# A searched step order replaced by another, for a chunked linear attention followed by a gated feed-forward layer

## The chip, the cores and the metric

The kernel runs on one core of one Trainium2 chip. The metric is the device time of one execution in microseconds. Before the change three runs took 177.21, 177.34 and 177.75 us; the median is 177.34 us.

## The reference

The first half is a recurrence over 768 positions, for 4 batches and 8 heads with 48 columns each. Each head keeps a 48 by 48 state, which decays by `w` at every position; the current position enters with its own factor `u`. The second half takes the result as 3072 rows of 384 columns through two matrix products with a gate between them.

```
for t in range(S):
    cur = einsum('bhd,bhe->bhde', u[None] * kt, vt)
    y[:, :, t] = einsum('bhd,bhde->bhe', rt, state + cur)
    state = w[None, :, :, None] * state + einsum('bhd,bhe->bhde', kt, vt)

h = x @ w_in                       # 3072 x 384 by 384 x 2048
g = where(h >= 1, h, where(h <= -1, 0, (h + 1) ** 2 / 4))
out = g @ w_out                    # 2048 x 384
```

## The kernel before

**Tiling.** The 768 positions are cut into 6 chunks of 128. The 4 batches make 2 pairs, so there are 12 groups `g` (chunk by pair), and each group has 2 units `j`, one per batch. A unit `n = 2g + j` is 128 positions of one batch with all 8 heads. Inside a chunk the recurrence is done by matrix products: R and K are scaled by powers of `w` (`Rs`, `Ks`, line 327), turned so that the columns lie on partitions, and multiplied into a 128 by 128 matrix per head (`A`, line 406). The matrix is masked to a triangle (`AT`, line 421, or on ACT and then POOL at lines 412 and 416) and multiplied with V (`Y`, line 446), and the state's part is added on PE (line 441). The term with `u` goes another way: `KU` (337), `RKU` (344), the row sum `usum` (357, or on ACT at 355 in one small instruction per head), `V2` (369), and `y` (468) adds it to `Y`. The state of a batch goes through `Sp` (432), `Tm` (476 or 484), `decay` (489, always POOL) and `sbf` (a copy to bf16).

**Turning.** Groups 0 to 2 turn R and K on PE (`T`, line 388, copied out by `TT`) and the result on PE (`X`, copied out by `xT`). From group 3 on this is done by DMA transposes, issued on SP's queue: `KRT` (line 398) for K and R, and `xT` (line 511) for a whole group.

**Feed-forward.** Each group has four quarters `q` of the 2048 inner columns. `mm1.g.q` (line 526) is 12 products of 256 columns; `relu` (534) and `square` (539) run on ACT, `gate` (544) on DVE, and `mm2.g.j.q` (line 554) is four products of 384 columns for one unit. `o` copies the sum out of PSUM, and `out` (587) stores it. The last unit is split in two (`rest`, `ends`) so that its store is short.

**Queues.** Five instruction streams run in order: PE, DVE, ACT, POOL and SP. SP issues all loads of R, K and V, all DMA transposes and nearly all stores; a step that waits there holds all behind it. POOL issues the weights: `w_in` in three transfers (line 290, columns 0 to 511, 512 to 1023, and the rest) and `w_out` in four (line 294, four tiles of 128 rows each), among its products.

**The order.** One string, `ORDER` (lines 35 to 100), lists all 715 steps; the program walks through it and appends each step's instructions to the queue of its engine. A step reads `name.args@engine:buffers~idles`. `@D`, `@P` and `@A` choose DVE, POOL or ACT where there is a choice. The digits after the colon choose the buffer: `h0` to `h2` are the PSUM tiles of two banks each that `A`, `mm1` and the transposes share, `bank0` and `bank1` the single banks. `~7` puts seven idle products of 128 columns (line 204, zeros times zeros) ahead of the step on PE; `warm.12.h.0` is twelve such products by themselves (line 608). Waits between engines follow from the order of the steps and the tiles that they share.

Of the kernel before, what the change touches and what calls it, by code (L numbers as in the profile page):

```python
# [40 lines left out]
Sp.2:1~2 load.K.2.0:2 V.1.1@A TT.3@A:0 V2.0.1@P AT.2.0:1 Tm.1@D Tm.2@D T.1:1~2 TT.1@A:1 Rs.2.0@P:2 Y.0:0~7 w_in.0
Sp.3:1~7 A.1:0 w_in.1 A.3:2 Ks.2.0@D:0 y.0:2 T.5:1 X.0:0~2 Tm.3@D V2.1.0@P:1 AT.1.1:0 AT.3.0:2 AT.1.0 Y.2:1~11
xT.0@D:0 T.4:0~4 usum.1.1@D Y.1:0 y.2:2 warm.2.h.2 Y.3:1 y.1:0 loadV.2.0:1 X.1:0~2 sbf.1@A V2.1.1@D TT.4@A:3 w_in.2
w_out.0 sbf.0@A xT.1@A V.2.0@D:3 A.4:0~4 sbf.3@A KU.2.0@D:1 RKU.2.0@P:0 mm1.0.0.0:2 mm1.0.0.1 TT.5@A:0 relu.0.0:1
y.3:0 AT.4.0:2 Sp.4:1~7 square.0.0:0 Tm.4@D:0 X.2:0~2 A.5:1~4 usum.2.0@D:1 gate.0.0:7 w_out.1 mm1.0.1.0:0 xT.2@A:1
# [20 lines left out]
gate.4.0:4 loadV.7.0:0 A.12:2 load.R.8.0:2 Tm.12@D:0 relu.4.2:1 KU.7.0@P:0 Sp.11:1 decay.9 KU.8.0@P:1 AT.12.0:0
square.4.2:0 sbf.10@A mm2.4.0.0:0 gate.4.1:5 mm1.4.3.-1:2 gate.4.2:0 A.13:0 V2.6.0@P:0 mm2.4.0.1 mm1.5.0.-1:1 out.2
Tm.11@D:1 sbf.9@A relu.4.3:1 AT.13.0:2 square.4.3:0 Y.12:1 Ks.7.0@P:0 mm2.4.0.2 KRT.K.7:0 relu.5.0:1 mm1.5.2.-1:0
square.5.0:1 y.12:0 relu.5.2:1 gate.4.3:8 square.5.2:0 Y.13:1 y.13 Rs.7.0@P:2 mm1.5.1.-1:2 mm2.4.0.3 decay.11
gate.5.0:2 RKU.7.0@P:1 o.4.0@A:0 relu.5.1:1 V.7.0@A:4 gate.5.2:9 usum.7.0@D:1 decay.12 KRT.R.7:0 mm2.4.1.0:1 mm2.4.1.1  # L70
sbf.11@A square.5.1:1 A.15:1 AT.15.0:3 A.14:0 mm2.4.1.2 Sp.13:0 RKU.8.0@P:0 V2.7.0@P:1 mm2.4.1.3 mm1.5.3.-1:1 o.4.1@A
Tm.13@D:1 load.K.9.0:0 xT.12:1 relu.5.3:0 Sp.14:1 AT.14.0:2 gate.5.1:8 loadV.8.0:0 square.5.3:0 Y.14:0 decay.13
Tm.14@D:1 mm1.6.0.-1:0 relu.6.0:0 out.4 mm1.6.1.-1:2 y.14:1 gate.5.3:3 square.6.0:1 Ks.8.0@P:1 Y.15:1 y.15 mm2.5.0.0:0
Rs.8.0@P:0 mm2.5.0.1 relu.6.1:1 Sp.15:1 usum.8.0@D:0 gate.6.0:6 square.6.1:0 KRT.K.8:0 KU.9.0@P:0 out.3 V.8.0@D:2
decay.14 mm1.6.2.-1:1 load.R.9.0:1 mm2.5.0.2 mm2.5.0.3 Ks.9.0@P:2 KRT.R.8:0 Tm.15@D:0 relu.6.2:0 square.6.2:1
o.5.0@A:0 sbf.12@A gate.6.1:0 mm1.6.3.-1:0 gate.6.2:4 xT.14:2 Sp.16:1 mm2.5.1.0:0 mm2.5.1.1 A.17:2 decay.15
load.K.10.0:0 relu.6.3:0 A.16:1 Tm.16@D:0 loadV.9.0:1 AT.17.0:2 square.6.3:0 mm2.5.1.2 mm2.5.1.3 AT.16.0:0
mm1.7.1.-1:2 o.5.1@A gate.6.3:3 decay.16 Y.16:1 RKU.9.0@P:0 sbf.15@A sbf.13@A V2.8.0@P:0 y.16:1 Y.17:0 load.R.10.0:2
relu.7.1:1 square.7.1:0 y.17 mm1.7.0.-1:1 relu.7.0:0 Sp.17:1 mm1.7.3.-1:0 mm2.6.0.0:0 gate.7.1:5 mm2.6.0.1 Tm.17@D:0
mm1.7.2.-1:2 mm2.6.0.2 Rs.9.0@P:2 usum.9.0@D:1 Ks.10.0@P:0 load.K.11.0:1 sbf.14@A KRT.K.9:0 out.5 KRT.R.9:1  # L80
square.7.0:1 xT.16:2 KU.10.0@D:1 RKU.10.0@P:1 gate.7.0:2 mm2.6.0.3 relu.7.3:0 square.7.3:0 decay.17 mm2.6.1.0:1
gate.7.3:8 V.9.0@A:0 relu.7.2:0 mm2.6.1.1 o.6.0@A:0 V2.9.0@P:0 A.19:1 A.18:0 Rs.10.0@P:1 mm2.6.1.2 mm2.6.1.3 AT.18.0:3
sbf.16@A square.7.2:0 o.6.1@A gate.7.2:9 Sp.18:0 mm1.8.0.-1:0 loadV.10.0:1 relu.8.0:0 KRT.R.10:0 Tm.18@D:0 Y.18:1
mm1.8.1.-1:2 mm2.7.0.0:0 KRT.K.10:0 mm2.7.0.1 square.8.0:1 AT.19.0:1 sbf.17@D y.18:0 loadV.11.0:0 mm2.7.0.2
usum.10.0@A:1 Y.19:1 gate.8.0:3 mm2.7.0.3 decay.18 y.19 o.7.0@D:1 A.20:0 A.21:1 mm2.7.1.0:1 xT.18:1 relu.8.1:0
AT.20.0:1 Sp.19:0 mm2.7.1.1 V.10.0@D:0 AT.21.0:3 mm1.8.2.-1:0 mm2.7.1.2 KU.11.0@P:0 square.8.1:1 sbf.18@A relu.8.2:0
gate.8.1:6 square.8.2:0 Ks.11.0@P:0 Tm.19@D:0 mm1.8.3.-1:1 out.6 Y.20:0 V2.10.0@D:0 mm2.7.1.3 mm1.9.1.-1:2 y.20:0
relu.8.3:0 gate.8.2:7 square.8.3:1 mm1.9.0.-1:0 o.7.1@D Y.21:1 mm2.8.0.0:0 y.21 load.R.11.0:2 Rs.11.0@P:1 gate.8.3:1
RKU.11.0@P:0 relu.9.1:1 relu.9.0:0 decay.19 square.9.0:0 gate.9.0:5 square.9.1:1 mm2.8.0.1 gate.9.1:8 usum.11.0@D:1
mm2.8.0.2 sbf.19@A KRT.R.11:0 KRT.K.11:0 mm2.8.1.0:1 mm2.8.0.3 mm1.9.2.-1:0 V.11.0@A:0 mm2.8.1.1 out.7 A.22:2  # L90
# [559 lines left out]
```

## Time and profile before

| | |
|---|---|
| median of the runs | 177.34 us |
| the profiled execution | 177.43 us |
| its span, first to last instruction | 175.7 us |
| mean granted TensorE clock | 0.997 |
| busy PE, DVE, ACT, POOL | 165.5, 140.4, 136.1, 103.5 us |
| HBM read and written | 20.45 and 4.72 MB |

The page gives each engine's busy time as a share of the span. Rows of the waits name the engine and line that waited, what let it go, the total, the number of times and the longest. Rows of a timeline are the start and the duration in us, the engine, the line, the operation, what it writes and reads, and the shape; a bracket names the idle time before it and what ended it. Rows of the chain are pieces of the path that ended last. "Landing" is the time from the issue of a DMA to its arrival.

### The profile page before, as it was taken

Reading aid. Unit: us, or ns where it says so; the run is one execution under the profiler, and the core shown is the slowest. Engines: PE = TensorE matmul, PEld = TensorE weight load, DVE = VectorE, ACT = ScalarE, POOL = GpSimd, SP = SyncE. Lnnn points to the kernel's source line nnn. Section 1 sums busy time; section 2 is a strip of 40 time slices with the busy share of each in tenths; the row PEclk is TensorE's granted clock in tenths of the full one; section 3 lists DMA queues with packets and bytes.
Section 4 is the critical chain, followed back from the end, with each engine's and each line's share of the span. In section 5 each row is a group of like instructions: output and inputs, shape, how many; then the busy total and the mean of one; then the engine's idle time right before and its main releaser. Section 6 shows DMA issues by size and latency. Waiting matters only on the chain.

```text
span 175.7 us, 4247 instructions
## 1 busy us (share of the span) xinstructions
PE 165.5 (94%) x1718; PEld 127.1 (72%) x1718; DVE 140.4 (80%) x181; ACT 136.1 (77%) x195; POOL 103.5 (59%) x85
## 2 busy tenths in 40 slices
...
GB/s 115 210 224 215 153 202 206 192 183 163 193 174 194 259 207 219 215 170 135 229 226 179 190 246 202 183 251 109 152 219 69 101 152 137 1 0 4 0 179 90
DMA packets 107367, 28.78 MB, mean 164 GB/s; under 512 B 100946, under 2 KB 106964, under 8 KB 107348
## 3 DMA queue, kind: packets, MB, share of 16 engines
...
q8 instruction: 13, 0.21, 0.5%
...
HBM read 20.45 MB, written 4.72 MB: 143 GB/s over the span
## 4 chain that ended last, share of the span: by engine, by line
PE 72%; DMA 16%; DVE 4%; ACT 2%; issue 2%; POOL 1%; SPq 1%; DVEq 0%
PE hp L526 29%; PE op L554 29%; DMA w_out_sb<-in_moe_w_out_dram 7%; DMA xT<-yy 5%; PE A L406 4%; DMA KT<-Ks 2%; PE Y L446 2%; DMA K<-in_k_dram 2%; PE Y L441 2%; PE Sp L432 2%; PE T L388 2%; DVE AT L421 1%; ACT TT L212 1%; POOL V L369 1%; PE Sp L204 1%
## 5 line engine op out<-in xcount | busy, mean ns | idle before, releaser
L526 PE MATMUL hp<-xT,w_in_sb 128*128 128x256 bf16 (+1 forms) x600 | 70.1, 268 | 2.0 <-DMA xT<-yy 1.6
L554 PE MATMUL op<-w_out_sb,gt 128*128 128x384 bf16 (+2 forms) x400 | 69.5, 320 | 0.4 <-DMA w_out_sb<-in_moe_w_out_dram 0.4
L544 DVE SCALAR_TENSOR_TENSOR gt<-sq,hp 128x1024 bf16<-128x1024 f32 x48 | 58.0, 1216 | 14.5 <-ACT sq L539 13.9
L526 PEld LDWEIGHTS <-w_in_sb 128*128 128x128 bf16 x600 | 55.6, 98 | 11.8 <-DMA xT<-yy 2.0
L534 ACT ACTIVATE pt<-hp 128x1024 f32<-128x1024 f32 x48 | 48.9, 1022 | 10.0 <-PE hp L526 9.4
L539 ACT ACTIVATE sq<-pt 128x1024 f32<-128x1024 f32 x48 | 50.6, 1058 | 2.0 <-DVE gt L544 0.9
L554 PEld LDWEIGHTS <-gt 128*128 128x128 bf16 x400 | 37.0, 98 | 20.5 <-issue 0.5
L421 DVE TENSOR_TENSOR AT<-A,umask 128x1024 bf16<-128x1024 f32 x22 | 26.6, 1218 | 3.1 <-PE A L406 3.0
L344 POOL TENSOR_TENSOR RKU<-R,KU 128x768 f32<-128x768 f32 (+1 forms) x11 | 18.4, 1677 | 11.1 <-DMA R<-in_r_dram 7.7
L369 POOL TENSOR_TENSOR V<-V,diag 128x768 f32<-128x768 bf16 (+1 forms) x11 | 15.9, 1442 | 8.5 <-DVE diag L357 4.7
L489 POOL TENSOR_TENSOR state<-Tm,wCm 128x384 f32<-128x384 f32 x16 | 16.7, 1041 | 6.8 <-DVE Tm L476 6.8
L327 POOL TENSOR_TENSOR Rs<-Wup,R 128x768 bf16<-128x768 f32 x8 | 14.6, 1820 | 4.8 <-issue 4.0
L327 POOL TENSOR_TENSOR Ks<-Wdn,K 128x768 bf16<-128x768 f32 x8 | 15.6, 1951 | 2.5 <-DMA KT<-Ks 1.9
L337 POOL TENSOR_TENSOR KU<-K,u_bc 128x768 f32<-128x768 f32 (+1 forms) x8 | 13.1, 1640 | 4.9 <-DVE RKU L344 3.0
L468 DVE TENSOR_TENSOR yy<-Y,V 128x384 bf16<-128x384 f32 x18 | 9.7, 554 | 6.3 <-PE Y L446 5.4
L212 ACT COPY oo<-op 128x384 f32<-128x384 f32 x18 | 8.6, 476 | 7.0 <-PE op L554 7.0
L212 ACT CAST V<-VF 128x768 bf16<-128x768 f32 (+1 forms) x10 | 7.0, 701 | 5.0 <-DMA VF<-in_v_dram 5.0
L446 PE MATMUL Y<-V,AT 128*128 128x48 bf16 x192 | 10.9, 183 | 0.0
L357 DVE TENSOR_REDUCE diag<-RKU 128x16 f32<-128x768 f32 (+1 forms) x13 | 10.6, 820 | 0.0
L446 PEld LDWEIGHTS <-AT 128*128 128x128 bf16 x192 | 9.5, 96 | 0.4
L212 ACT CAST state_bf<-state 128x384 bf16<-128x384 f32 x18 | 9.0, 509 | 0.0
L476 DVE TENSOR_TENSOR Tm<-Sp,state 128x384 f32<-128x384 f32 x16 | 8.7, 549 | 0.0
...
## 6 DMA issues: line engine op xcount, KB each, us to landing
...
w_out_sb<-in_moe_w_out_dram POOLq DMA_DIRECT2D x4, 384.0 KB, 10.2
...
```

The lines of the kernel that those rows point to most:

```text
L212: nc.scalar.copy(out, in_) if e == "A" else engines[e].tensor_copy(out, in_)
L327: engines[e].tensor_mul(of_unit(dst, j0, j1)[:, :, :, :D], rep(tab, j1 - j0), of_unit(tiles[what, g], j0, j1))
L344: engines[e].tensor_mul(of_unit(tiles["RKU", g], j0, j1), of_unit(tiles["R", g], j0, j1), of_unit(tiles["KU", g], j0, j1))
L369: engines[e].tensor_mul(tiles["V2", g][:, hs, :], tiles["V", g][:, hs, :], tiles["diag", g][:, hs].unsqueeze(2).to_broadcast([P, hs.stop - ...
L421: nc.vector.tensor_mul(t.rearrange("p i n t -> p (i n) t"), tiles.pop(("A", n)).rearrange("p i n t -> p (i n) t"), umask.unsqueeze(1).to_b ...
L446: nc.tensor.matmul(t[:, 2 * p + i, :], tiles["AT", n][:, i, p, :], tiles["V", g][:, j * H + 2 * p + i, :], start=(c == 0), stop=True, skip ...
L489: nc.gpsimd.tensor_mul(states[(g % BP) * UNITS + j], tiles.pop(("Tm", n)), wCm)
L526: nc.tensor.matmul(hp[:, f, cols], w_in_sb[:, i, n0 : n0 + P], tiles["xT", g][:, units, i, :], start=(i == 0), stop=(i == nK - 1), skip_gr ...
L534: nc.scalar.activation(tiles["pt", g, q], tiles["hp", g, q], AF.Relu, bias=0.5, scale=0.5)
L539: nc.scalar.activation(tiles["sq", g, q], tiles.pop(("pt", g, q)), AF.Square, bias=0.0)
L544: nc.vector.scalar_tensor_tensor(out=gt, in0=tiles.pop(("sq", g, q)), scalar=1.0, in1=tiles.pop(("hp", g, q)), op0=ALU.min, op1=ALU.max)
L554: nc.tensor.matmul(t, tiles["gt", g, q][:, f, j * P : (j + 1) * P], w_out_sb[:, n, cols], start=(n == 0), stop=(n == nF - 1),)
```

## The change

Only the string `ORDER` differs. It has the same 715 steps, but for the idle products: `warm.12.h.0` and two `warm.2.h.2` become `warm.6.h.1` and two `warm.2.h.0`, and the idle products ahead of steps become 81 where there were 80, at other steps. In all there are 91 instead of 96. The steps stand in another order on every queue. 43 steps have another engine, and 306 have another buffer number. The new engines, by step:

- from DVE to POOL: KU.1.0, KU.1.1, RKU.1.1, KU.2.0, Ks.3.0, Rs.3.0, Rs.4.0, KU.4.0, RKU.6.0, V2.10.0
- from POOL to DVE: KU.0.0, RKU.0.0, KU.0.1, KU.5.0, RKU.11.0, V2.11.0
- from ACT to DVE: TT.0, V.1.1, sbf.0, TT.5, V.3.0, sbf.5, sbf.10, sbf.11, sbf.14, o.5.0, usum.10.0, o.8.0, o.10.1
- from DVE to ACT: xT.0, usum.1.1, V.2.0, sbf.2, V.4.0, o.2.0, V.8.0, sbf.17, o.7.0, o.7.1, V.10.0, o.9.0, o.11.0
- from POOL to ACT: V2.1.0

The order of the first loads on SP's queue before is K.0.0, K.0.1, K.1.0, V.0.0, R.0.0, K.1.1, R.1.0, V.0.1, R.1.1, R.0.1, R.2.0, V.1.0, V.1.1, K.2.0. After it is V.1.0, V.0.0, K.0.0, R.0.0, K.0.1, K.1.0, R.0.1, R.1.0, K.1.1, V.0.1, R.1.1, V.1.1, R.2.0, K.2.0. The diff, cut to the start, the last weights and the places around four transposes:

```diff
 ORDER = """
-warm.12.h.0 bcu:1 load.K.0.0:1 lw u_bc@D load.K.0.1 bcw:0 Wdn_p:0 load.K.1.0:0 KU.1.0@D:0 loadV.0.0:1 Ks.0.0@D:1
-KU.0.0@P:1 load.R.0.0:0 Wup_p wcol:1 load.K.1.1 load.R.1.0:2 V.0.0@A:2 loadV.0.1 load.R.1.1 wCm Ks.1.0@D:2 Rs.0.0@D:1
-RKU.0.0@P:1 T.0:1~2 Ks.1.1@D TT.0@A:3 usum.0.0@D:1 load.R.0.1 Rs.1.0@D:0 Ks.0.1@D A.0:1 AT.0.1:2 Wup KU.1.1@D
...
-load.K.3.0:0 mm2.0.0.0:1 load.R.3.0:1 Tm.5@D:1 square.0.2:0 w_out.2 Ks.3.0@D:0 mm1.0.3.-1:2 w_out.3 decay.5 gate.0.2:1
...
-o.1.0@A:0 AT.6.0:2 Sp.7:1 mm1.2.2.-1:2 Tm.7@D:1 Rs.5.0@P:2 decay.7 Tm.6@D:0 Y.6:1 relu.2.0:1 Y.7:0 y.6:0 mm1.2.1.-1:1
-y.7 xT.6:1 relu.2.2:0 Ks.5.0@P:0 load.K.6.0:0 square.2.0:0 decay.6 mm2.1.1.0:0 gate.2.0:9 relu.2.1:1 mm2.1.1.1
-square.2.1:1 sbf.6@A mm2.1.1.2 mm2.2.0.0:1 Ks.4.0@P:1 Rs.4.0@D:0 gate.2.1:2 mm2.1.1.3 mm1.3.1.-1:0 mm1.3.2.-1:1
...
-o.2.1@A mm2.3.0.3 V2.4.0@P:0 Y.8:0 y.8:0 A.10:1 o.3.0@A:1 Y.9:1 Rs.6.0@P:0 A.11:2 load.K.7.0:2 sbf.8@A y.9 loadV.6.0:1
-xT.8:1 Sp.10:0 Tm.10@D:0 RKU.6.0@D:0 load.K.8.0:1 V2.5.0@P:1 decay.10 mm2.3.1.0:1 mm2.3.1.1 AT.11.0:1 Sp.9:0 mm2.3.1.2
-V.6.0@A:1 mm2.3.1.3 sbf.7@A KRT.R.6:1 mm1.4.0.-1:2 AT.10.0:0 o.3.1@A Y.10:1 Tm.9@D:1 usum.6.0@D:1 Y.11:0 relu.4.0:1
...
+loadV.1.0:1 lw loadV.0.0:0 load.K.0.0:0 load.R.0.0:2 bcu:0 u_bc@D load.K.0.1 load.K.1.0:2 load.R.0.1 bcw:1 KU.0.0@D:0
+Wdn_p:0 warm.6.h.1 wcol:0 V.0.0@A:4 V.1.0@A:2 Ks.0.0@D:2 load.R.1.0:0 Wup_p wCm load.K.1.1 RKU.0.0@D:1 Rs.0.0@D:1
+Rs.0.1@D loadV.0.1 KU.0.1@D T.0:1 TT.0@D:0 Ks.0.1@D load.R.1.1 Ks.1.0@D:0 loadV.1.1 Wdn usum.0.0@D:1 A.0:2~2
+Rs.1.0@D:0 KU.1.0@P:1 RKU.1.0@P:0 Ks.1.1@D AT.0.1:0 Sp.2:0~7 Rs.1.1@D KU.1.1@P load.R.2.0:1 Tm.2@D V.1.1@D T.2:1~4 Wup
+V.0.1@A T.1:0 RKU.0.1@P Sp.1:1 TT.2@A:1 usum.0.1@D Sp.3:0~4 RKU.1.1@P Tm.1@D Tm.3@D usum.1.0@D:0 Sp.0:1 load.K.2.0:2
+AT.0.0 Rs.2.0@P:1 A.2:1 w_in.0 TT.1@A:2 Tm.0@D AT.2.0:1 A.1:2~8 Y.0:1~16 Ks.2.0@D:2 V2.0.0@D:1 y.0:2 warm.2.h.0
+V2.1.0@A:0 AT.1.1:2 Y.2:0~2 w_in.1 AT.1.0 T.3:0~2 V2.0.1@P T.4:2 TT.3@A:3 TT.4@A:1 y.2:0 X.0:1 xT.0@A:2 Y.1:0~2
+usum.1.1@A A.3:1 y.1:2 T.5:0~8 w_in.2 KU.2.0@P:1 X.1:1~4 AT.3.0:3 X.2:0 mm1.0.0.0:2 xT.1@A w_out.0 TT.5@D:2
+RKU.2.0@P:1 xT.2@A:0 Y.3:1~4 w_out.1 V2.1.1@D y.3:2 loadV.2.0:1 A.5:1 AT.5.0:1 V.2.0@A:2 sbf.1@A mm1.0.0.1
+load.K.3.0:1 relu.0.0:1 A.4:0 Sp.5:0 X.3:1 AT.4.0:3 mm1.0.1.0:1 xT.3@A mm1.0.1.1 Tm.5@D:0 square.0.0:0 mm1.1.1.-1:0
+relu.0.1:0 load.R.3.0:1 square.0.1:1 w_out.2 Sp.4:1~7 sbf.0@D relu.1.1:1 decay.5 usum.2.0@D:0 Y.4:0~7 gate.0.0:8
+V2.2.0@P:1 Ks.3.0@P:1 mm1.1.0.-1:2 loadV.3.0:1 gate.0.1:2 y.4:1 square.1.1:1 load.K.4.0:2 Tm.4@D:1 gate.1.1:3
+mm1.0.2.-1:1 Y.5:0~4 X.4:1 mm1.0.3.-1:0 y.5:1 relu.1.0:0 w_out.3 square.1.0:0 gate.1.0:9 relu.0.2:0 KU.3.0@D:0
...
+AT.6.0:1 decay.6 o.1.0@A:1 gate.2.3:5 Y.6:1 load.R.5.0:0 KU.4.0@P:0 y.6:0 Y.7:0 load.K.5.0:0 load.R.4.0:2 mm1.2.2.-1:1
+relu.2.0:0 Rs.5.0@P:2 mm2.1.1.0:1 mm2.1.1.1 square.2.0:1 mm1.2.1.-1:2 y.7 gate.2.0:4 V.5.0@A:2 mm2.1.1.2 KU.5.0@D:1
+relu.2.2:1 sbf.5@D square.2.2:0 xT.6:1 decay.7 gate.2.2:7 relu.2.1:0 mm2.1.1.3 loadV.4.0:1 load.K.6.0:2 RKU.5.0@P:0
+o.1.1@A out.0 RKU.4.0@D:1 mm1.3.1.-1:0 Rs.4.0@P:0 square.2.1:1 KRT.K.4:0 gate.2.1:9 relu.3.1:1 Ks.5.0@P:0 usum.4.0@D:1
...
+sbf.7@A KU.6.0@P:1 mm2.3.0.1 loadV.6.0:0 A.10:2 load.K.7.0:0 A.11:1 gate.3.3:6 Rs.6.0@P:2 Y.9:1 mm2.3.0.2 y.9
+mm2.3.0.3 RKU.6.0@P:0 xT.8:2 AT.10.0:3 o.3.0@A:1 mm2.3.1.0:1 out.2 AT.11.0:2 mm2.3.1.1 Sp.10:0 Tm.10@D:1 mm2.3.1.2
+KU.7.0@P:1 KRT.R.6:0 mm2.3.1.3 o.3.1@A Sp.9:0 Tm.9@D:0 KRT.K.6:0 mm1.4.0.-1:1 V.6.0@A:1 Y.10:1 Y.11:0 decay.10
...
+square.5.2:1 loadV.7.0:1 usum.7.0@D:0 o.4.0@A:0 gate.5.0:7 mm2.4.1.1 Y.13:0 sbf.11@D V.7.0@A:3 gate.5.2:9 A.15:2 y.13
+load.R.8.0:0 A.14:0 AT.15.0:2 relu.5.1:1 square.5.1:1 AT.14.0:1 mm2.4.1.2 mm2.4.1.3 o.4.1@A V2.7.0@P:1 load.R.9.0:2
+Sp.13:0 mm1.5.3.-1:2 xT.12:1 Y.14:1 Tm.13@D:0 relu.5.3:0 Y.15:0 Rs.8.0@P:2 decay.13 gate.5.1:2 y.14:0 mm1.6.0.-1:0
...
+KRT.K.10:1 usum.10.0@D:0 mm2.7.1.0:1 square.8.0:1 Y.19:0 gate.8.1:4 loadV.11.0:0 mm2.7.1.1 gate.8.0:9 A.21:2 A.20:0
+y.19 mm2.7.1.2 relu.8.3:0 sbf.16@A Rs.11.0@P:1 Sp.19:0 load.K.11.0:2 V.10.0@A:2 sbf.17@A mm2.7.1.3 square.8.3:1
+AT.20.0:1 xT.18:2 mm1.8.2.-1:0 Tm.19@D:0 o.7.1@A Y.20:0 relu.8.2:0 gate.8.3:0 V2.10.0@P:0 mm1.9.1.-1:1 AT.21.0:3
+KRT.R.11:1 mm1.9.0.-1:2 square.8.2:1 y.20:0 decay.19 V.11.0@A:1 Ks.11.0@P:2 relu.9.1:1 KRT.K.11:1 relu.9.0:0 Y.21:1
+gate.8.2:1 KU.11.0@P:0 mm2.8.0.0:0 y.21 mm2.8.0.1 sbf.18@A mm2.8.0.2 mm2.8.1.0:1 mm2.8.0.3 square.9.1:1 RKU.11.0@D:1
+mm2.8.1.1 usum.11.0@D:0 A.22:0 out.7 gate.9.1:8 A.23:1 mm2.8.1.2 AT.22.0:1 square.9.0:1 AT.23.0:3 o.8.0@D:0 out.6
...
 """
```

More of the change, by code (lines that the diff above doesn't have):

```diff
@@ L41 @@
[L41 to L45, printed above, removed]
@@ L66 @@
[L66 to L70, printed above, removed]
@@ L71 @@
[L71 to L90, printed above, removed]
@@ new lines @@
+V2.2.0@P:1 Ks.3.0@P:1 mm1.1.0.-1:2 loadV.3.0:1 gate.0.1:2 y.4:1 square.1.1:1 load.K.4.0:2 Tm.4@D:1 gate.1.1:3
+mm1.0.2.-1:1 Y.5:0~4 X.4:1 mm1.0.3.-1:0 y.5:1 relu.1.0:0 w_out.3 square.1.0:0 gate.1.0:9 relu.0.2:0 KU.3.0@D:0
+xT.4@D:2 relu.0.3:1 Rs.3.0@P:2 square.0.2:1 sbf.3@A sbf.2@A square.0.3:0 mm2.0.0.0:0 mm1.1.3.-1:2 gate.0.2:5
+gate.0.3:7 relu.1.3:0 mm2.0.1.0:1 decay.4 mm2.0.1.1 mm2.0.0.1 square.1.3:1 KRT.K.3:0 RKU.3.0@P:0 mm1.1.2.-1:1
+mm2.0.0.2 mm2.0.0.3 mm2.0.1.2 gate.1.3:0 o.0.0@A:0 relu.1.2:1 X.5:0 warm.2.h.0 square.1.2:0 V.3.0@D:2 mm2.0.1.3 xT.5@D
@@ new lines @@
+o.1.1@A out.0 RKU.4.0@D:1 mm1.3.1.-1:0 Rs.4.0@P:0 square.2.1:1 KRT.K.4:0 gate.2.1:9 relu.3.1:1 Ks.5.0@P:0 usum.4.0@D:1
+square.3.1:0 out.1 KRT.R.4:0 mm2.2.0.0:1 mm2.2.1.0:0 Ks.6.0@P:1 mm1.3.2.-1:1 mm2.2.0.1 KRT.R.5:1 mm2.2.1.1
+usum.5.0@D:0 mm1.3.0.-1:2 relu.3.2:0 square.3.2:1 mm2.2.0.2 relu.3.0:1 mm2.2.1.2 gate.3.1:9 gate.3.2:0 V2.5.0@P:1
+square.3.0:1 mm2.2.0.3 mm2.2.1.3 A.8:1 gate.3.0:8 o.2.0@A:0 sbf.6@A KRT.K.5:1 load.R.6.0:1 V.4.0@A:1 AT.8.0:1
+V2.4.0@P:0 o.2.1@A mm1.3.3.-1:0 Sp.8:0 relu.3.3:0 A.9:2 Tm.8@D:0 Y.8:1 mm2.3.0.0:0 square.3.3:0 AT.9.0:0 y.8:1 decay.8
@@ new lines @@
+Rs.7.0@P:1 AT.12.0:2 Sp.12:1 mm1.4.3.-1:1 gate.4.1:2 A.13:0 mm2.4.0.1 relu.4.3:1 sbf.9@A Tm.12@D:0 Y.12:1 gate.4.2:5
+load.K.8.0:2 AT.13.0:1 KRT.K.7:1 y.12:1 mm1.5.0.-1:2 mm1.5.2.-1:0 decay.11 RKU.7.0@P:0 decay.12 mm2.4.0.2 square.4.3:1
+gate.4.3:0 mm2.4.0.3 relu.5.0:1 KU.8.0@P:0 square.5.0:0 KRT.R.7:1 sbf.10@D mm2.4.1.0:1 mm1.5.1.-1:1 relu.5.2:1
+square.5.2:1 loadV.7.0:1 usum.7.0@D:0 o.4.0@A:0 gate.5.0:7 mm2.4.1.1 Y.13:0 sbf.11@D V.7.0@A:3 gate.5.2:9 A.15:2 y.13
+load.R.8.0:0 A.14:0 AT.15.0:2 relu.5.1:1 square.5.1:1 AT.14.0:1 mm2.4.1.2 mm2.4.1.3 o.4.1@A V2.7.0@P:1 load.R.9.0:2
```

49 lines of the change are left out of this document (25 added, 24 removed).

## The prediction

> **What bounds the kernel now.** I read the page first, then the waits of the TensorE alone, then the stages, then the chain in order of time.
>
> ```profile
> span 175.7 us, 4247 instructions
> PE 165.5 (94%) x1718; PEld 127.1 (72%) x1718; DVE 140.4 (80%) x181; ACT 136.1 (77%) x195; POOL 103.5 (59%) x85
> ```
> The profiled execution took 177.43 us, 1.73 more than its span. The sum is made against 177.43, which stands 0.09 above the median of the runs (177.34). A busy PE need not be a useful one, so PE's own waits come next (total, times, longest), then the stages (busy PE, weight loads, DVE, ACT, POOL, then the granted clock, the DMA share and GB/s):
>
> ```profile
> PE hp L526 <- DMA xT<-yy: 1.6, 1, 1.6
> PE op L554 <- DMA w_out_sb<-in_moe_w_out_dram: 0.4, 1, 0.4
> PE hp L526 <- DVE AT L421: 0.3, 1, 0.3
> PE A L406 <- DMA KT<-Ks: 0.2, 1, 0.2
> ```
> ```profile
> 58.00:78.00 20.00, 18.34 (x180) 12.95 (x179) 19.03 (x22) 12.42 (x17) 16.41 (x10) 1.00 1.27 214
> 78.00:100.00 22.00, 21.66 (x254) 17.29 (x253) 18.96 (x22) 19.87 (x23) 18.96 (x14) 1.00 0.91 193
> 100.00:128.00 28.00, 27.76 (x297) 20.64 (x296) 23.89 (x29) 24.76 (x56) 23.25 (x17) 1.00 0.96 193
> ```
> From 78 to 128 us PE idles 0.58 us in 50, and only the stage from 58 to 78 shows a hole. So PE bounds the kernel, an order cannot remove its work, and what it can win is the waits, or an earlier start of the dense stream. The chain in order of time names the places:
>
> ```profile
> 15.58 0.85 PE T L388 x8
> ...
> 17.98 0.45 PE T L388 x8
> ...
> 20.81 0.17 PE X L501 x3
> ...
> 22.46 0.21 PE Y L446 x8
> ...
> 30.34 11.53 DMA w_out_sb<-in_moe_w_out_dram
> ...
> 45.02 1.31 PE hp L526 x12
> 46.33 0.65 PE op L554 x4
> 46.98 0.55 PE A L406 x16
> ...
> 48.94 0.17 PE Sp L432 x4
> ...
> 53.46 3.78 DMA xT<-yy
> 57.28 2.78 PE hp L526 x24
> ...
> 72.46 4.53 DMA xT<-yy
> 77.03 1.48 PE hp L526 x12
> ...
> 123.67 3.99 DMA KT<-Ks
> ```
> These also give the units in which PE's order is counted below: a layer-1 step (mm1) 1.31, a layer-2 step (mm2) 0.65, A 0.55, Sp 0.17, X 0.17, and Y 0.21 for its eight products without a state; with a state it has twelve, an estimate of 0.38.
>
> **Part 1: the start.** PE's first dense products, and the rows of DVE and POOL that carry the first weights:
>
> ```profile
> 24.24 1.51 PE L526 MATMUL hp<-xT,w_in_sb 128*128 128x128 bf16 x24
> ```
> ```profile
> 5.77 1.34 DVE L337 TENSOR_TENSOR KU<-K,u_bc 128x384 f32<-128x384 f32 x1 [0.15 <-DMA K<-in_k_dram]
> ```
> ```profile
> 12.12 1.00 POOL L344 TENSOR_TENSOR RKU<-R,KU 128x384 f32<-128x384 f32 x1 [1.73 <-DMA R<-in_r_dram]
> 13.08 1.41 POOL L416 TENSOR_SCALAR_AFFINE_SELECT AT<-AT 128x1024 bf16<-128x1024 bf16 x1
> 15.45 1.82 POOL L327 TENSOR_TENSOR Rs<-Wup,R 128x768 bf16<-128x768 f32 x1
> 17.20 1.71 POOL L290 DMA_DIRECT2D w_in_sb<-in_moe_w_in_dram  x2
> ```
> ```profile
> DMA to landing us min/median/max: 6.5/8.4/9.0
> ```
> The last row is of the three w_in transfers; the first of them is the 6.5, since mm1.0.0.0 ran at 24.24 without a wait for it, and 17.20 + 6.5 = 23.7. The new order puts more in front of that issue. The third load on SP's queue (K.1.0) let its reader go at 5.77 and the tenth (R.0.1) at 12.12, so a half load lands every (12.12 − 5.77)/7 = 0.91 us. In the new queue R.1.1 is the eleventh (13.0), and R.2.0, twice as long, lands at about 15.8. POOL then has RKU.1.1 to 14.0, the triangle select AT.0.0 to 15.4, Rs.2.0 from 15.8 to 17.6, and w_in.0 goes out at 17.6 and lands at 24.1. So mm1.0.0.0 starts at about 24.1, 0.14 earlier than now, held by the weights. Behind it lies other PE work: Y.3 (0.21) and A.4 (0.55) come after it in the new order, X.2 (0.17) before it, and three more idle products follow it, at 0.45/8 each. Start: −0.14 + 0.21 + 0.55 − 0.17 + 0.17 = **+0.6**. Bounds: −0.4 if the idle products and A.4 fall into waits, +1.7 from the clock (below).
>
> The other moved steps of the start give ACT V2.1.0 and usum.1.1, eight small instructions each, and take two TT copies from it. The nearest row of the small ones is the sum that ACT does now:
>
> ```profile
> 124.93 0.23 ACT L355 ACTIVATE RKU<-RKU 128x48 f32<-128x48 f32 x1
> ```
> ```profile
> L421 DVE TENSOR_TENSOR AT<-A,umask 128x1024 bf16<-128x1024 f32 x22 | 26.6, 1218 | 3.1 <-PE A L406 3.0
> L212 DVE COPY xT<-X 128x384 bf16<-128x384 bf16 x3 | 1.1, 350 | 0.7 <-PE X L501 0.7
> L212 ACT COPY TT<-T 128x1024 bf16<-128x1024 bf16 x6 | 6.1, 1012 | 2.6 <-PE T L388 2.6
> ```
> Sixteen at 0.23 are 3.7 us against 2.0 saved, so 1.7 more. I cost this at nothing, since ACT's TT copies stand waiting 2.6 us for T; without that cover xT.1 comes up to 1.7 later and mm1.0.0.1 with it. DVE's copy of a T block (TT.0, TT.5) has no row: it is between 0.35 (its copy of 384 columns) and 1.22 (the masked product over 1,024), and I take 0.8, by the columns. It is not later than the 1.01 that ACT takes.
>
> **Part 2: the last weights.** w_out.3 goes out right behind w_out.2 now (30.34) and lands 11.53 later; PE waits 0.4 for it (41.87 less 41.5, when mm1.1.2 in front of it ends). In the new order decay.5, V2.2.0 and Ks.3.0 stand between them on POOL. From AT.1.0, which leaves POOL at about 20.5 (an estimate: it waits for ACT's copy of A.1, about 19, and takes 1.41), the queue holds V2.0.1 1.0, w_in.2 0.8, KU.2.0 1.8, w_out.0 0.8, RKU.2.0 1.8, w_out.1 and w_out.2 1.6, decay.5 1.0, V2.2.0 1.5, Ks.3.0 1.8 (whole products by Rs at 15.45, issues by w_in): 12.1, so w_out.3 issues near 32.6.
>
> ```profile
> L369 POOL TENSOR_TENSOR V<-V,diag 128x768 f32<-128x768 bf16 (+1 forms) x11 | 15.9, 1442 | 8.5 <-DVE diag L357 4.7
> L489 POOL TENSOR_TENSOR state<-Tm,wCm 128x384 f32<-128x384 f32 x16 | 16.7, 1041 | 6.8 <-DVE Tm L476 6.8
> ```
> ```profile
> DMA to landing us min/median/max: 9.6/10.2/11.5
> ```
> This row is of w_out: landing at 42.2 to 44.1. mm2.0.0.3 has the same mm1 and mm2 steps ahead of it in both orders, so it is due near 41.5 again. The stall becomes 0.7 to 2.6. If the transfer is as quick as w_in.0's 6.5, because fewer stand ahead of it, there is none. I take the quickest w_out landing, 0.7 against 0.36: **+0.34**; bounds −0.36 and +2.2.
>
> **Part 3: the transposes.** From the end of the second Y to the landing of xT it is 57.28 − 52.48 = 4.80 for group 3 and 77.03 − 71.77 = 5.26 for group 4, by the chain and
>
> ```profile
> 52.48 1.47 PE L526 MATMUL hp<-xT,w_in_sb 128*128 128x256 bf16 x12
> ...
> 71.77 0.40 PE L406 MATMUL A<-RT,KT 48*128 48x128 bf16 x8
> ```
> The cover is the PE work between that Y and the first mm1 that needs it. Now group 3 has one mm1 and five mm2, 4.56, so 0.24 is idle; group 4 is idle for 1.62. In the new order group 3 has two mm1 and four mm2, 5.2; group 4 six mm2 and two Sp, 4.24. Two groups with ample room have less: group 6 (two A, two mm2, Sp, mm1.5.3, Y.14, Y.15) 4.6, group 9 (three mm2, two A, Sp, mm1.8.2, Y.20) 4.9. With 4.80 for all, the stalls are 0, 0.56, 0.2, 0; with 5.26 they are 0.06, 1.02, 0.66, 0.36. The middle transpose is quicker than the two in the chain:
>
> ```profile
> xT<-yy SPq DMA_TRANSPOSE x9, 3.3
> ```
> 3.3 against 3.78 and 4.53, so 4.3 from Y, which even group 4 nearly covers. I therefore take 4.80 for group 4, which issues into the same loads as now, and 4.3 for the others: 0.56 instead of 1.86, **−1.3**; bounds −1.86 and +0.24. KRT.K.11 is waited for 0.24 now. In the new order fourteen PE steps, 9.2 us, lie between Sp.19 and A.22, and what follows on Sp.19 (Tm 0.5, decay 1.0, Ks.11 1.8, landing 4.0) is 7.3: **−0.24**, or 0. The 0.3 in front of mm1.4.3 stays: A.12, one mm2 and one Sp lie ahead of it as before. POOL gains four whole steps net, some 7 us, less a half; 3.6 of it falls before 45 us, and the fullest stage has 18.96 of 22.
>
> **Sum.** 177.43 + 0.6 + 0.34 − 1.3 − 0.24 = 176.83, less 0.09: **176.7 us**. The tail holds the same stores.
>
> **The clock.** Eight transposes took 0.85 us at 15.58 and 0.45 at 17.98, while the stages show the granted clock at 1.00; the start runs at half speed until about 17.7. The Trainium skill, "TensorE: Matmul & The Clock Gate", Part 1, has the array at half rate until a free-running window of about 3.4 us has been busy. The two rows agree with the halving; it speaks against this change, whose twelve opening products become six that stand after the tables.
>
> **The rivals.** (a) *w_out.3 late*, the slower side: POOL issues it at 32.6, the transfer takes the 11.5 of its slowest row, and mm2.0.0.3 waits until 44.1; it decides from a landing later than 42.8. For it: three steps moved in front; against: fewer transfers ahead. Price 2.2 in place of 0.34: 178.6. (b) *All transposes late*: y.13 stands behind gate.5.2 and y.19 behind two gates on DVE, which is 95% busy from 58 to 78; with 5.0 to 5.26 for every group the stalls are 1.3 to 2.1 instead of 0.56, so 177.4 to 178.2. Against it: seven of nine landed without a wait of PE. (c) *Full speed comes late*: by the two rows, 1.7 us of full-speed PE work takes 3.4; if full speed comes some 3.4 us later, 1.7 is lost: 178.4. For it: fewer opening products; against it: 81 products before steps fill gaps. (d) *Every cover suffices*: −1.86 − 0.24, and Parts 1 and 2 cost nothing: 177.43 − 2.1 − 0.09 = 175.2.
>
> **How the numbers follow.** A measurement of this kernel tells 0.3% (0.53 us) from no change, so faster is below 176.8 and slower above 177.9. Forecast 0.42 (176.0 to 177.5: faster 0.26, same 0.14, slower 0.02), (a) 0.14 slower, (b) 0.18 (same 0.10, slower 0.08), (c) 0.08 slower, (d) 0.18 faster. Together faster 0.44, same 0.24, slower 0.32. The range runs from a little under (d), 174.8, to 179.0, above (a).
>
> **What would show it.** w_in.0 issued at 17 to 18 us and mm1.0.0.0 at 24 to 24.6; a PE wait on w_out near 42 of 0.4 to 1; a PE wait on xT below 1 us near 76, none near 57; none on KT near 127. It is wrong if mm1.0.0.0 comes after 25.5, if PE waits for an engine from 58 us on, or if the stalls of groups 6 and 9 exceed 1 us.

## The result, and the profile after

The changed kernel took 175.31 us (median of four runs, 174.49 to 175.69) against 177.51 (177.21 to 177.75) of the kernel before beside it: a ratio of 0.987, with an interval of 0.983 to 0.991. The forecast was 176.7 with a range of 174.8 to 179.0; the result is faster by 1.3% and stands nearest to rival (d), "every cover suffices", at 175.2.

The profiled execution took 175.69 us, the slowest of the four, against 177.43 before. Its page, its waits of PE from 24 us on, and its stages:

```profile
span 174.0 us, 4223 instructions
PE 163.9 (94%) x1713; PEld 126.0 (72%) x1713; DVE 137.3 (79%) x177; ACT 135.5 (78%) x187; POOL 107.8 (62%) x88
```
```profile
PE hp L526 <- DMA w_in_sb<-in_moe_w_in_dram: 0.8, 1, 0.8
PE Sp L432 <- DVE xT L212: 0.6, 1, 0.6
PE hp L526 <- DVE AT L421: 0.3, 1, 0.3
```
```profile
58.00:78.00 20.00, 20.00 (x214) 14.41 (x212) 16.56 (x20) 13.86 (x18) 17.47 (x11) 1.00 1.06 222
78.00:100.00 22.00, 21.66 (x247) 17.48 (x246) 20.45 (x27) 20.09 (x24) 19.60 (x14) 1.00 0.99 169
```
The waits on xT by DMA, on w_out and on KT are gone; the hole of 1.66 us in the stage from 58 to 78 is filled. From 24 us on two waits are new: on w_in at 24 us, as Part 1 had it, and one of 0.6 ahead of a state product, which no part had. Their places in PE's timeline (start, duration; the bracket is the idle time ahead of the row):

```profile
24.16 0.84 PE L526 MATMUL hp<-xT,w_in_sb 128*128 128x128 bf16 x12 [0.82 <-DMA w_in_sb<-in_moe_w_in_dram]
41.23 2.11 PE L554 MATMUL op<-w_out_sb,gt 128*128 128x384 bf16 x12
43.54 0.81 PE L554 MATMUL op<-w_out_sb,gt 128*128 128x384 bf16 x4
44.92 0.33 PE L432 MATMUL Sp<-V,Ks 128*128 128x96 bf16 x4 [0.56 <-DVE xT L212]
75.56 1.47 PE L526 MATMUL hp<-xT,w_in_sb 128*128 128x256 bf16 x12
```
The row at 41.23 holds mm2.0.0.3 without a wait. The same places before, with mm2.0.0.3 at 41.90, mm2.0.1.3 at 43.55 and mm1.4.0 at 77.03:

```profile
41.90 1.46 PE L554 MATMUL op<-w_out_sb,gt 128*128 128x384 bf16 x8 [0.36 <-DMA w_out_sb<-in_moe_w_out_dram]
43.55 1.46 PE L554 MATMUL op<-w_out_sb,gt 128*128 128x384 bf16 x8
73.95 1.46 PE L554 MATMUL op<-w_out_sb,gt 128*128 128x384 bf16 x8
77.03 1.48 PE L526 MATMUL hp<-xT,w_in_sb 128*128 128x256 bf16 x12 [1.62 <-DMA xT<-yy]
```

**Where the time went.** At two points both orders have done exactly the same PE steps: when mm2.0.1.3 ends and when mm1.4.0 starts. The start of a step's row, with 0.65 added for mm2.0.1.3 (43.54 + 0.65 = 44.19), cuts every trace into three stretches:

| execution | mm2.0.1.3 ends | mm1.4.0 starts | span | stretch 2 | stretch 3 |
|---|---|---|---|---|---|
| before | 44.20 | 77.03 | 175.7 | 32.83 | 98.67 |
| before, second execution | 44.47 | 76.00 | 174.7 | 31.53 | 98.70 |
| after | 44.19 | 75.56 | 174.0 | 31.37 | 98.44 |
| after, second execution | 44.23 | 74.90 | 173.3 | 30.67 | 98.40 |

Start: nothing. Stretch 2: −1.46. Stretch 3: −0.23. Together −1.69, the whole of 175.7 − 174.0. The second executions (below) give −0.24, −0.86 and −0.30, −1.4 together. Most of the gain stands in the stretch where PE waited for transposes, which looked like proof of Part 3. The experiments show that it is at most half of the story.

### The profile page after: what moved, and what is told of

It is laid out like the page before. It is cut to its first block, busy times and chain, and to the rows that moved or that the text cites. A ratio compares the mean times of both kernels' runs of the same rounds, so it can differ in the third digit from the quotient of the medians.

```text
span 174.0 us, 4223 instructions
## 1 busy us (share of the span) xinstructions
PE 163.9 (94%) x1713; PEld 126.0 (72%) x1713; DVE 137.3 (79%) x177; ACT 135.5 (78%) x187; POOL 107.8 (62%) x88
## 4 chain that ended last, share of the span: by engine, by line
PE 75%; DVE 7%; DMA 6%; ACT 5%; SPq 3%; issue 2%; POOL 1%; ACTq 0%; POOLq 0%
PE op L554 33%; PE hp L526 31%; PE A L406 4%; DMA w_in_sb<-in_moe_w_in_dram 3%; ACT sq L539 3%; SPq L304 3%; DMA R<-in_r_dram 2%; PE Y L446 2%; DVE gt L544 2%; PE Y L441 2%; DVE AT L421 2%; PE Sp L432 2%; ACT pt L534 2%; POOL Rs L327 1%; PE T L388 1%
## 5 line engine op out<-in xcount | busy, mean ns | idle before, releaser
L526 PE MATMUL hp<-xT,w_in_sb 128*128 128x256 bf16 (+1 forms) x600 | 69.1, 268 | 1.1 <-DMA w_in_sb<-in_moe_w_in_dram 0.8
L327 POOL TENSOR_TENSOR Rs<-Wup,R 128x768 bf16<-128x768 f32 x10 | 19.0, 1896 | 8.4 <-DMA R<-in_r_dram 7.4
L344 POOL TENSOR_TENSOR RKU<-R,KU 128x768 f32<-128x768 f32 (+1 forms) x11 | 17.9, 1635 | 1.8 <-DVE KU L337 0.9
L369 POOL TENSOR_TENSOR V<-V,diag 128x768 f32<-128x768 bf16 (+1 forms) x10 | 14.1, 1410 | 7.9 <-ACT V L212 7.4
L337 POOL TENSOR_TENSOR KU<-K,u_bc 128x768 f32<-128x768 f32 (+1 forms) x9 | 14.9, 1654 | 4.8 <-DMA K<-in_k_dram 4.7
L327 POOL TENSOR_TENSOR Ks<-Wdn,K 128x768 bf16<-128x768 f32 x9 | 16.4, 1826 | 1.0 <-DMA K<-in_k_dram 1.0
L212 ACT CAST V<-VF 128x768 bf16<-128x768 f32 (+1 forms) x12 | 8.9, 747 | 1.2 <-PE Y L446 1.2
L441 PE MATMUL Y<-state_bf,RT 128*128 128x96 bf16 x72 | 8.3, 204 | 0.0
```

Of the source, the lines that this page charges most:

```text
L212: nc.scalar.copy(out, in_) if e == "A" else engines[e].tensor_copy(out, in_)
L327: engines[e].tensor_mul(of_unit(dst, j0, j1)[:, :, :, :D], rep(tab, j1 - j0), of_unit(tiles[what, g], j0, j1))
L337: engines[e].tensor_mul(of_unit(tiles["KU", g], j0, j1), of_unit(tiles["K", g], j0, j1), rep(u_bc, j1 - j0))
L344: engines[e].tensor_mul(of_unit(tiles["RKU", g], j0, j1), of_unit(tiles["R", g], j0, j1), of_unit(tiles["KU", g], j0, j1))
L526: nc.tensor.matmul(hp[:, f, cols], w_in_sb[:, i, n0 : n0 + P], tiles["xT", g][:, units, i, :], start=(i == 0), stop=(i == nK - 1), skip_gr ...
```

## Experiments

Four kernels ran on one chip, four on a second, four on a third, each group beside its own runs of the kernel before. Single runs of the kernel before lie up to 1.1 us apart on the first (176.23 to 177.30), 3.8 on the second and 3.2 on the third (176.22 to 179.45), so half a per cent needs the medians.

**1 and 2. Half of the change each.**

The first has the new steps up to mm1.2.3 and the old ones behind (two buffers renumbered), the second the old up to there and the new behind (five renumbered). The seams, against the new and the old order:

```diff
 xT.5@D Ks.4.0@P:2 o.0.1@A Sp.6:0
-mm1.2.3.-1:2 Tm.6@D:0 relu.2.3:1 Sp.7:0 mm2.1.0.0:1 ...
+KRT.R.3:1 load.R.5.0:2 load.K.5.0:1 mm2.1.0.0:1 mm1.2.3.-1:2 gate.1.2:1 ...
```
```diff
 mm2.1.0.0:1 decay.4 gate.1.3:7
-mm1.2.3.-1:2 gate.1.2:1 o.0.1@A mm2.1.0.1 ...
+load.K.4.0:2 Ks.4.0@P:2 o.0.1@A Sp.6:0 mm1.2.3.-1:2 Tm.6@D:0 ...
```


> The new order and engines for every step up to the product mm1.2.3 (about 45 us), and the old order and engines for all steps behind it. Theory (the middle's transposes carry the gain): the start costs PE about 0.5 us by the two traces and the old middle stalls on xT of groups 3 and 4 as before, so 177.3 to 178.2 us. Rival (the start carries the gain): 175.0 to 176.0. Rival (the gain is spread over all moves): about 176.4.

> The other half: the old order and engines up to mm1.2.3, the new ones behind it. Theory (the middle's transposes carry the gain): no PE wait on a transpose from 57 us on, 174.7 to 175.7 us, not slower than the whole change. Rival (the start carries it): 177 or more. Rival (spread): about 176.4.

Measured: 180.72 us, ratio 1.021 (1.017 to 1.026), and 181.75, ratio 1.029 (1.025 to 1.033). Both halves are slower than either whole. PE and DVE in the first, then PE and POOL in the second:

```profile
70.05 0.48 PE L432 MATMUL Sp<-V,Ks 128*128 128x96 bf16 x4 [2.92 <-DVE oo L212]
69.44 0.56 DVE L212 COPY oo<-op 128x384 f32<-128x384 f32 x1 [3.57 <-DMA out_dram<-oo]
```
```profile
58.08 2.72 PE L554 MATMUL op<-w_out_sb,gt 128*128 128x384 bf16 x8 [3.16 <-DVE yy L468]
54.20 1.80 POOL L327 TENSOR_TENSOR Ks<-Wdn,K 128x768 bf16<-128x768 f32 x1 [9.01 <-DMA K<-in_k_dram]
```
The seam makes them. In the first, o.1.0 was renumbered at the seam, and o.2.0 on DVE now needs the buffer that the store out.0 empties, which the old order issues late (65.34); DVE stands 3.57 us for it. In the second, load.K.4.0, which the new start has far ahead, stands at the seam with its reader Ks.4.0 right behind; POOL stands 9.01 us for it, and V2, y and PE follow. So the halves can't be priced by themselves, none of the registered ranges was met, and the two runs say only that an order's transfers, its buffers and its products belong together.

**3. Group 4's cover alone.** In the old order Y.9 goes ahead of two mm2 and of o.3.0. Its bank 1 holds mm2.3.0 until o.3.0 has copied it out, so the moved Y.9 takes bank 0.

```diff
-mm2.3.0.1 mm2.3.0.2 usum.5.0@D:0 o.2.1@A mm2.3.0.3 V2.4.0@P:0 Y.8:0 y.8:0 A.10:1 o.3.0@A:1 Y.9:1 ... y.9
+mm2.3.0.1 o.2.1@A V2.4.0@P:0 Y.8:0 y.8:0 A.10:1 Y.9:0 mm2.3.0.2 mm2.3.0.3 o.3.0@A:1 ... y.9 usum.5.0@D:0
```


> The old order with one local edit: in group 4 the two layer-2 steps mm2.3.0.2 and mm2.3.0.3 (with o.3.0) are moved behind Y.9, and usum.5.0 behind y.9 on DVE, as the new order has them. The cover between Y.9 and mm1.4.0 grows by 1.3 us, and y.9 goes 0.9 earlier on DVE. Theory (cover of single transposes): the PE wait of 1.6 us on xT falls below 0.4 and the time to 175.9 to 176.5. Rival (the wait only moves, to another transpose or to A): 177.0 to 177.6.

Measured: 178.13 us, ratio 1.007 (1.0045 to 1.0095). The wait on xT is gone, and a wait ahead of Y.9 has come:

```profile
71.43 0.20 PE L441 MATMUL Y<-state_bf,RT 128*128 128x96 bf16 x1 [1.78 <-DVE yy L468]
...
71.80 2.52 PE L554 MATMUL op<-w_out_sb,gt 128*128 128x384 bf16 x8
...
75.10 1.64 PE L554 MATMUL op<-w_out_sb,gt 128*128 128x384 bf16 x8
```
Y.9 now needs the bank that y.8 empties. Worse, in this execution the eight products behind the gap take 2.52 us where eight take 1.46 otherwise, and PE is back at full rate only at about 75.4. The slow products cost some 1.5 us, nearly as much again as the gap. They are not in every execution: three of the six runs have a mean granted clock of 0.99 and take 178.29 to 178.60 us, the other three have 0.999 or 1.0 and take 177.49 to 177.97, still above 176.93. The theory fails; the rival's mechanism holds, the wait moved, but to a place and a price that it did not have. And since the edit changed a bank too, the run doesn't tell what the cover alone would be worth.

**4. The new order on the old engines.** The 43 steps go back to the engines that they had; nothing else differs.

```diff
-KU.0.0@D:0 ... TT.0@D:0 ... V2.1.0@A:0 ... xT.0@A:2 ... V.3.0@D:2 ...
+KU.0.0@P:0 ... TT.0@A:0 ... V2.1.0@P:0 ... xT.0@D:2 ... V.3.0@A:2 ...
```


> The new order with all 43 steps back on their old engines. Theory (the order and not the engines removes the waits): 175.0 to 176.2 us, the start perhaps later by a few tenths. Rival (the engines carry the gain): 176.8 to 177.8.

Measured: 195.0 us, ratio 1.10 (1.097 to 1.104), far above both registered ranges. The engines are no ornament: this order, as it stands, can't be had without them. Which of the 43 matter, the run doesn't tell.

**5 and 6. xT out of the way, in both orders.** From group 3 on mm1 reads 256 columns of w_in where it read xT, so nothing waits for that transpose (which still runs); the results of these groups are other numbers.

```diff
-                    hp[:, f, cols], w_in_sb[:, i, n0 : n0 + P], tiles["xT", g][:, units, i, :],
+                    hp[:, f, cols], w_in_sb[:, i, n0 : n0 + P], tiles["xT", g][:, units, i, :] if g < X_DMA else w_in_sb[:, i, : UNITS * P],
```


> The old order, but from group 3 on the layer-1 products read the first 256 columns of the first weights in place of the transposed result xT, so no product can wait for a transpose of the result (the output of those groups is left wrong; the transposes are still made). Theory (the waits on xT carried the gain): the two gaps, 0.24 and 1.62 us, go, and nothing takes their place: 174.9 to 175.7 us, about the time of the whole change. Rival (another wait steps in, on KT, AT or a gate): 176.2 or more.

> The new order with the same replacement of xT from group 3 on. Theory (the new covers all suffice): no gain, within 0.4 us of the new kernel, 174.7 to 175.6. Rival (the transposes still cost the new order something): 174.3 or less.

Measured: old order 176.93 us, ratio 0.999 (0.997 to 1.002); new order 175.79, ratio 0.994 (0.991 to 0.997). In the old order the wait that was put at 1.6 us is worth nothing on the median. Its rival holds: another wait steps in, on Y for a copy on ACT, which run 11 explains.

```profile
77.03 0.20 PE L441 MATMUL Y<-state_bf,RT 128*128 128x96 bf16 x1 [0.74 <-ACT oo L212]
```
The new order doesn't gain from it either: its ratio is not below the 0.987 and 0.990 of the changed kernel, so its covers seem to suffice. The changed kernel itself did not run on this chip.

**7 and 8. The new start.** In one, w_in.0 goes ahead of Rs.2.0 on POOL, and V.3.0 to ACT ahead of o.0.0; in the other, 24 idle products between 24 and 44 us are left out, 22 ahead of steps and the last `warm.2` (the expectation prices 22).

```diff
-AT.0.0 Rs.2.0@P:1 A.2:1 w_in.0 ... o.0.0@A:0 ... V.3.0@D:2
+AT.0.0 w_in.0 Rs.2.0@P:1 A.2:1 ... V.3.0@A:2 o.0.0@A:0 ...
```
```diff
-Y.3:1~4 ... Sp.4:1~7 ... Y.4:0~7 ... Y.5:0~4 ... warm.2.h.0 square.1.2:0
+Y.3:1 ... Sp.4:1 ... Y.4:0 ... Y.5:0 ... square.1.2:0
```


> The new order with two local edits at the two waits that its PE still shows: the issue of w_in.0 goes ahead of Rs.2.0 on POOL, which stood idle there for 1 us, and V.3.0 goes from DVE to ACT, ahead of o.0.0, so that xT.5 no longer stands behind it. Theory (the weights' landing holds the first product, by 0.82 us, and the cast holds Sp.6, by 0.56): 1.0 to 1.4 us faster than the new kernel, 173.8 to 174.4. Rival (the start is paced by ACT and the middle by the order as a whole): within 0.4 us of it, or slower where a PE gap above 1.7 us opens.

> The new order without the 22 idle products that stand in front of Y.3, Sp.4, Y.4 and Y.5 and the last two behind X.5, all of them after the first dense product. They are 22 x 0.056 = 1.2 us of PE time. Theory (PE waits for ACT and DVE between 24 and 45 us, and the idle products fill those waits): no change, within 0.4 us of the new kernel. Rival (they lie on PE's path): 0.8 to 1.2 faster. Rival (they keep the array at full speed): slower by 0.5 or more, and products at half rate near 33 us.

Measured: 175.84 us, ratio 0.992 (0.990 to 0.995), and 175.34, ratio 0.993 (0.990 to 0.996). Neither ratio can be told from that of the changed kernel (0.990 on the third chip), so the theory of run 7, 1.0 to 1.4 us faster, fails, and that of run 8, no change, holds as far as the ratios tell. In the first the w_in wait goes and X.5 waits for o.0.0 behind V.3.0 (the profiled execution is the slowest of its eleven, 177.38); in the second mm2.0.1.3 ends at 43.63, 0.6 earlier, although mm1 waits for gates at 30.7 and 34.2:

```profile
PE X L501 <- ACT oo L212: 1.1, 1, 1.1
```
```profile
PE hp L526 <- DVE gt L544: 0.9, 2, 0.7
```

**9 and 10. Both kernels again.** Exact copies, for a base line and a second profile.

> The changed kernel itself, unaltered, beside the kernel before on this chip, as the base line for the two variants below and as a second profile. Theory: 175.0 to 175.8 us, ratio to the kernel before 0.987 to 0.993; the profile again shows no wait of PE on xT above 0.3 us near 76 us, and one of about 0.8 on w_in near 24. Rival: the gain belonged to the first chip; then the ratio is above 0.995.

> The kernel before itself, unaltered, as a second profile. Theory: the wait of PE on the transposed result (xT) near 76 us is there again at 1.3 to 2.0 us, and PE idles about 2.5 us in all from 25 us on. Rival: the transpose lands at another time in each execution; then this wait comes out below 0.8 us, or another group has it, and the first profile's 1.6 us was one sample.

Measured: new 175.84 us, ratio 0.990 (0.987 to 0.994); the copy of the old, 176.98, ratio 0.998 (0.994 to 1.001), with the old kernel at 177.37 beside them. The gain holds when measured again. The same row of the old kernel in its second profile, then of the new:

```profile
76.00 1.48 PE L526 MATMUL hp<-xT,w_in_sb 128*128 128x256 bf16 x12 [0.57 <-DMA xT<-yy]
```
```profile
74.90 1.47 PE L526 MATMUL hp<-xT,w_in_sb 128*128 128x256 bf16 x12
```
The wait on which Part 3 was built is 0.57 us here and was 1.62: it was one sample, and the rival registered for this run holds. The old order's waits on w_out and on KT, 0.36 and 0.24 in the first profile, are in no row of the second. Of the new kernel's two new waits, the one on xT at 44.9 is absent, and w_in costs 1.4 instead of 0.8.

**11. All transposes out of the way in the old order.** As in 5, and A and the state's part of Y read the tile of unit 5 for R and K from group 3 on. The results of these groups are other numbers.

```diff
-        if g < T_DMA:
-            return tiles["TT", n][:, "RK".index(what) * NP + p, :]
+        if True:
+            return tiles["TT", min(n, T_DMA * UNITS - 1)][:, "RK".index(what) * NP + p, :]
```


> The old order. From group 3 on the matrices A and the state's part of Y read the tile of R and K that PE turned for unit 5, and mm1 reads the first columns of w_in in place of xT, so no product of PE waits for any DMA transpose; the transposes are still issued, and the outputs of groups 3 to 11 are other numbers. Theory that the landing of the transposes as a whole carries the gain: 175.0 to 175.6 us, ratio 0.986 to 0.993. Rival, that the waits on DVE, ACT and POOL carry it and step in when the transposes are out of the way: 176.3 us or more, ratio 0.996 or above, with PE waits on Y, op or hp for DVE or ACT of 0.5 us or more.

Measured: 176.62 us, ratio 0.995 (0.992 to 0.999): 0.75 of the 1.53 us that the new order gains on this chip (177.37 − 175.84). Against the copy of the old order (176.98) it is 0.36 of 1.14, and run 5 had nothing, so the transposes are worth something between nothing and half of the gain. The ratio lies between the theory's range and the rival's; the time and the wait that steps in are the rival's. On PE and on ACT:

```profile
77.67 0.20 PE L441 MATMUL Y<-state_bf,TT 128*128 128x96 bf16 x1 [0.82 <-ACT oo L212]
```
```profile
76.00 0.83 ACT L212 CAST V<-VF 128x768 bf16<-128x768 f32 x1 [4.28 <-DMA VF<-in_v_dram]
76.74 0.51 ACT L212 CAST state_bf<-state 128x384 bf16<-128x384 f32 x1
77.15 0.47 ACT L212 COPY oo<-op 128x384 f32<-128x384 f32 x1
```
Y.10 needs the bank that o.3.1 (77.15) empties; o.3.1 stands on ACT behind sbf.7 and V.6.0, and V.6.0 stands 4.28 us for its load. The row was there before too, hidden under the wait on xT, here with the load's issue on SP's queue:

```profile
69.16 1.63 SPq L304 DMA_DIRECT2D VF<-in_v_dram  x1
76.24 0.83 ACT L212 CAST V<-VF 128x768 bf16<-128x768 f32 x1 [4.65 <-DMA VF<-in_v_dram]
```
And in the changed kernel:

```profile
65.70 1.84 SPq L304 DMA_DIRECT2D VF<-in_v_dram  x1
75.59 0.48 ACT L212 COPY oo<-op 128x384 f32<-128x384 f32 x1 [2.29 <-PE op L554]
75.97 0.84 ACT L212 CAST V<-VF 128x768 bf16<-128x768 f32 x1
```
The new order issues that load 3.46 us earlier and sets V.6.0 behind o.3.1. So near 76 us the old order had two late landings, xT for mm1.4.0 and V for the bank of Y.10, within a microsecond of each other. In its second execution both are a microsecond earlier (mm1.4.0 at 76.00, V.6.0 at 75.26). Removing the first exposes the second; the new order removes both. By stretches, as in the table above:

| execution | stretch 2 | stretch 3 |
|---|---|---|
| old order, xT free (5) | 30.81 | 99.48 |
| old order, all free (11) | 30.80 | 99.52 |
| new order, xT free (6) | 30.93 | 98.41 |
| new order, 24 idle products fewer (8) | 30.99 | 98.38 |

With the transposes free, the old order's stretch 2 is as short as the new one's second execution (30.67), and its stretch 3 is 0.8 longer than its own was with the wait on xT: that is the wait for o.3.1. The new order's stretch 3 lies between 98.33 and 98.44 in both of its own profiles and in those of 6, 8 and 12; in that of 7 it is 99.09, with a wait of 0.54 for a gate at 94 us. That the V load makes the rest of the gain is read from these rows; no run moved V.6.0 alone, and that stays open.

**12. Both edits of the start together**, with V.3.0 left on DVE.

> The changed kernel with two edits: w_in.0 is issued ahead of Rs.2.0 on POOL, 1.8 us earlier, with V.3.0 left on DVE where the new order has it, and the 22 idle products ahead of Y.3, Sp.4, Y.4, Y.5 and the second warm.2 are gone. Theory: the wait of 0.8 us on w_in at 24 us goes, and 22 idle products at about 0.05 us are 1.1 us of PE in the start, part of it hidden in waits; together 174.0 to 174.9 us, 0.5 to 1.3 below the changed kernel run beside it. Rival: what PE wins there it waits for ACT and DVE before 45 us, and the time is within 0.4 us of the changed kernel.

Measured: 175.53 us, ratio 0.990 (0.986 to 0.994), beside 175.84 and 0.990 of the changed kernel. Its rival holds: mm2.0.1.3 ends 0.4 earlier, at 43.78, and 0.50 ahead of Sp.6 and 0.36 on a KRT transpose take it back. Of the versions tried none beats the changed kernel by more than can be measured.

## Why the prediction was right where it was, and wrong

The sign came out, and the time lay in the range, but 1.4 us under the forecast. The sum had −0.60 for the profiled execution; it was −1.74 (175.69 − 177.43). Faster was the likeliest outcome of the prediction, with 0.44; rival (d), whose time comes nearest, had 0.18 of that. Its condition on the covers came true, but its time is met by luck: it leaves out the 0.73 below, and has Parts 1 and 2 at nothing where they cancel.

- **Part 1, +0.6: right, in part by luck.** w_in.0 was issued at 18.20 (predicted 17.6) and mm1.0.0.0 ran at 24.16 (24.1), held by the weights: the issue was 0.6 late, and the landing, 5.9 instead of 6.5, made it up. From there to the end of mm2.0.1.3 it took 20.03 us against 19.96 before, or 19.43 without the wait on w_out (0.53 from start to start): +0.60, less 0.08, is +0.52. One unit in it was wrong, though the sum doesn't show it: A was taken at 0.55 from a row of the chain with x16, but a step is one product for each of 8 heads, so these are two steps, 0.28 each. With 0.28 the sum is +0.35; what fills the 0.17 that are left is in no row of the waits.
- **Part 2, +0.34: wrong, −0.53.** w_out.3 was issued at 33.15 (predicted 32.6), but the landing was shorter than the quickest row of before: the step "I take the quickest w_out landing" failed. w_out.3 was in place when PE reached mm2.0.0.3 at 41.23 + 0.65 = 41.88, so it took 8.7 us at most. The case in which "there is none" came, and rival (a) fell. The old order's second execution, too, has 8.2 as its quickest w_out landing and no wait on it: the row that I took and the wait of 0.36 were one sample. Below, the four w_out transfers of the changed kernel:

```profile
DMA to landing us min/median/max: 8.0/8.8/10.7
```
- **A term that was missing, +0.73 in this execution.** Sp.6 waits at 44.92 for the copy of xT.5, which stands on DVE behind V.3.0, one of the 43. I had costed the moved casts on DVE at nothing. In the second execution the cast takes 0.67 instead of 1.38 and the wait isn't there (below).
- **Part 3, −1.3 and −0.24: a size too small, and the price not what it seemed.** From start to start the two waits on xT were 1.78 (73.95 + 1.30 to 77.03) and 0.24, and both went: −2.02; another 0.17 of stretch 2 is in no row of the waits. The covers sufficed at 4.23 us (71.33, the end of Y.9, to 75.56), under the 4.80 that I took as the lag of group 4; the landing isn't a constant of the group (5.26 in the old order's first execution, 4.21 in its second, 71.79 to 76.00). Stretch 3 shortened by 0.23, as much as the wait on KT; but that wait is absent from the old order's second execution, and its stretch 3 is no shorter (98.70), so what shortens the stretch stays open. (Between Sp.19 and A.22 stand twelve steps and not fourteen; their 9.2 us are right.) But the step "1.62 is what xT costs here" failed: it is 0.57 in another execution, and free of it altogether the old order gains nothing (5). A wait is worth only what lies between it and the next one, and V.6.0's load stood right behind. The new order also moves that load and that cast, which I had not looked at: they belonged to no wait of PE in the profile of before. By the rows of run 11, though by no run of its own, this is why it gains where the old order does not.
- **The clock, rival (c): fell.** PE's half rate ended 3 us earlier, not later. It has to be read from the products, since the granted clock is 1.00 there in both: four products in 0.39 are full rate, four in 0.62 half. The changed kernel, then the one before:
```profile
14.21 0.62 PE L388 MATMUL T<-ident,Rs 128*128 128x128 bf16 x4
14.84 0.39 PE L204 MATMUL Sp<-zeros 128*128 128x128 bf16 x4
```
```profile
15.80 0.63 PE L388 MATMUL T<-ident,Rs 128*128 128x128 bf16 x4
...
17.81 0.39 PE L388 MATMUL T<-ident,Ks 128*128 128x128 bf16 x4
```
- **Rival (b), all transposes late: fell**; groups 6 and 9 show no wait, though by A's true size their covers are only 4.2 and 4.5 us (91.95 to 96.13 and 127.96 to 132.42) where I had 4.6 and 4.9.

The terms as measured, 0.52 − 0.53 + 0.73 − 2.02 − 0.17 − 0.23, sum to −1.70, and the span fell by 1.7. The forecast's −0.60 was short because Part 2's sign was wrong (0.87) and Part 3 was sized too small (0.9 with the 0.17), less the 0.73 that was missing.
